# Another order of issue for a fused LSH-attention and token-mixing kernel, with a table of offsets

## The chip, the cores and the metric

The kernel runs on one core of a Trainium2 chip. The metric is device time in microseconds: 776.6 us before the change, the median of three runs (773.48, 776.6 and 777.08). The profile was taken from a further execution, which took 773.32 us.

The core has four engines that compute: TensorE (PE; PEld is its weight load), VectorE (DVE), ScalarE (ACT) and GpSimd (POOL). SyncE (SP) issues all transfers. Each engine runs its own queue in the order in which the program was written, and engines wait for each other by semaphores.

## The reference

Attention for 4 batches, 8 heads, 768 positions and width 64, in which a query sees only the keys whose six hash bits agree with its own; then, by batch, a token-mixing layer on the 512 joined channels.

```python
q_bucket = sum((q @ proj > 0) * powers);  k_bucket = sum((k @ proj > 0) * powers)
scores = where(q_bucket == k_bucket, q @ k.T / sqrt(64), -1e9)
x = softmax(scores) @ v                              # (4, 8, 768, 64) -> (4, 768, 512)
theta = x @ w_theta
y = w_tok_r @ (x * cos(theta)) + w_tok_i @ (x * sin(theta))     # over the 768 positions
u = x + y
out = u + relu(u @ w_ch)
```

## The kernel before

The work is cut into 96 attention steps, one for each batch, pair of heads and slice of 128 queries, and a mixing stage for each batch. Everything is first written down as some 3,300 small operations (`op(name, prio, ...)`, each with its engines, its rough length, what it depends on, and the buffers it holds). `issue_all` then plays a clock forward: whenever an engine is free in the model, it gives it the ready operation with the lowest `key`, and calls the function that writes the instructions. So the key, the model's lengths and the buffer counts decide the order in each engine's queue, and some operations (`qkl`, `p2`, `sign`, `zl` and others) go to whichever of two engines comes first.

One head of one attention step is this chain. TensorE makes the scores (`dst` for batch 0, one head at a time, from `nat`, `rows` and `kb`; `st` for the others, both heads, from `hl`). DVE takes the maximum (`vmax`, L800) and two small factors (L803, L806), ACT the exponential (`pf`, L810) and its 16-bit high half (`p1`, L816), POOL or DVE the low half (`p2`, L822). SP issues a transposing transfer (`turn`, L826, `pt<-pp`), and TensorE multiplies the result with the values (`pv`, 18 matmuls of 64 or 65 columns, `ps<-vv,pt`). The sums are divided into `x` (`norm`, L871).

Mixing for a batch transposes x (`xtr`, L921), projects it with `w_theta` (`proj`), turns the angles into sines on ACT (`trig`, L987 and L988), multiplies them with x on DVE (`zf`, tile `f`, L999), splits the products z into two halves (`zh`, `zl`, L1010), and runs the token mixing on TensorE (`y`, 36 matmuls for each of six output slices, `ps<-z,wtk`), which needs the z of all positions. Then come `u`, another projection with `w_ch`, and the store. The mixing of one batch runs among the attention steps of the next one; that of batch 0 thus starts after the 24 steps of batch 0.

The token weights (`raw`, then `wtk` at L520) and channel weights are loaded and split along the way. For batches 1 to 3 each pair of heads has its own preparation: q and k are split into two parts (`qkh`, and `qkl` at L631, tile `hl`), and their hash bits are made by TensorE, ACT and DVE, and turned into signs (`sign`, L707, tile `rows`) on DVE or POOL.

Where TensorE would have nothing to do in the model, and the model's clock is below `FILL`, the planner writes a filler, a 128x512 matmul of the constant tile `idle`, into the queue (`idle = e == "PE" and now < FILL ...`, L261, and `filler`, L354). Its result is not read. A filler in the queue runs whether the work behind it is ready or not.

Of the kernel before, what the change touches and what calls it, by code (L numbers as in the profile page):

```python
# [31 lines left out]
def lsh_attention_moe_kernel(ctx: ExitStack, tc: tile.TileContext, qk, wt, v, consts, w_theta, w_ch, out):  # L32
# [73 lines left out]
    WAKE = {"ACT": 45, "DVE": 37, "PE": 58, "POOL": 105, "SP": 40}  # L106
    AFTER = {"pv": 94, "vall": 70, "y": 17}
    WIDE = {"proj", "bits"}
    SHARED = {"qkl", "p1", "p2", "zf", "zh", "zl", "mag", "wlow", "whigh", "wmul", "wl", "vv2", "wtl"}

    class Slot:
        def __init__(self, pool):
# [26 lines left out]
    def issue_all():  # L139
# [1 line left out]
            return EXPORT(locals_())  # L141
        left = {}
        for i, o in enumerate(ops):
            o.key = (round(o.prio, 4), i)
            for sl in o.slots:
                left.setdefault(sl, []).append(o)

# [92 lines left out]
        while todo:  # L240
            progress = False
            for e in START:
# [165 lines left out]
    def widened(srcs, n, nm, tag, prio, stage="x", by=1.0):  # L408
        m = len(srcs)
        t = {}  # L410
        k_ = m * n / 512
        sx, sz = Slot(stage), Slot(tag)

        def load():
            t["w64"] = w64 = mp.tile([P, m, n, 2], U32, tag=sx.tag, name=f"w64_{nm}")
            for i, src in enumerate(srcs):
                dma(w64[:, i].rearrange("p n two -> p (n two)"), src)
            fs = mp.tile([P, 2, m, n], F32, tag=sz.tag, name=f"wf_{nm}")
            t["f"], t["sg"] = (fs[:, i].rearrange("p m n -> p (m n)") for i in range(2))
            t["w"] = fs[:, 0]  # L420
            w2 = w64.rearrange("p m n two -> p (m n) two")
            t["lo"], t["hi"] = w2[:, :, 0], w2[:, :, 1]

        def low():
            DVE.tensor_scalar(t["f"].bitcast(U32), t["lo"], 29, 0x40000000, ALU.logical_shift_right, ALU.bitwise_xor)

        def high():
            fu = t["f"].bitcast(U32)
            DVE.scalar_tensor_tensor(fu, t["hi"], 3, fu, ALU.logical_shift_left, ALU.bitwise_xor)

        a = op("wload", prio, on("SP", [(350, P * n * 8)] * m, load), slots=[sx, sz])
# [35 lines left out]
    def prep_wtok(to, prio):  # L467
# [4 lines left out]
        for r in range(2):  # L472
            def piece(r=r):
# [20 lines left out]
                a = op("wload", WL0 + WLS * (2 * to + r), on("SP", [(350, P * S * 8)], load), slots=[sw_])  # L494
# [40 lines left out]
    def prep_v(b, hp, prio):  # L535
# [42 lines left out]
        r = op("vload", prio + LV0, on("SP", [(410, 2 * S * D * 4)], load), slots=[svb])  # L578
# [16 lines left out]
    def prep_qk(b, hp, G, g):  # L595
# [10 lines left out]
                dma(t["nat"][:, i], qk[b, hp, :, i])  # L606

        if direct:
            hs.append(op("qkload", G + QKL, on("SP", [(330, 2 * S * D * 4)] * 2, whole), slots=[sh]))
        for i in range(0 if direct else 2):  # L610
            def half(i=i):
                sn = Slot("nat")
                u = {}

                def load():
                    u["nat"] = ap_.tile([P, S], F32, tag=sn.tag, bufs=1, name=f"nat{i}_{b}_{hp}")
                    dma(u["nat"], qk[b, hp, :, i])

                def high(e):
                    def go():  # L620
                        if "hl" not in t:
# [11 lines left out]
                ld = op("qkload", G + QKL + 0.02 * i, on("SP", [(330, 2 * S * D * 4)], load), slots=[sn])  # L633
# [102 lines left out]
    def step(g, b, hp, i, t, vt, po):  # L736
# [22 lines left out]
                        mm(st[j][:, k0:k1], l, r, n == 0, n == len(terms) - 1)  # L759

        if g < SH:
            a = [op("dst", g + DS * j, on("PE", 1750, lambda j=j: scores([j])), t["ready"], [ss[j]] + t["slots"]) for j in range(2)]
        else:
            a = [op("dst" if b == 0 else "st", g, on("PE", 1900 if b == 0 else 1600, lambda: scores([0, 1])), t["ready"], ss + t["slots"])] * 2

        def mcs():
            if "mc" not in mc:
                mc["mc"] = ap_.tile([P, 3, 2], F32, tag=smc.tag, bufs=1, name=f"mc_{nm}")
                order.extend((1, 0) if joint and ss[0].idx > ss[1].idx else (0, 1))
            return mc["mc"]  # L770

        order = []
# [1 line left out]
        def vmax2():  # L774
            a, c = sorted(x.idx for x in ss)
            DVE.tensor_reduce(mcs()[:, 0], psum[:, 2 * a * BANK : 2 * (2 * c - a) * BANK].rearrange("p (j n) -> p j n", j=2)[:, :, :S], AX.X, ALU.max, negate=True)

        def factor2():
# [5 lines left out]
        joint = g >= MG  # L784
        if joint:
            mj = op("vmax", g + VM, on("DVE", 1665, vmax2), [a[0], a[1]], ss + [smc])
            mj = op("factor", g + VM, on("DVE", 65, factor2), [mj], [smc])
            mj = op("shift", g + VM, on("DVE", 125, shift2), [mj], [smc])
        for j in range(2):
            def head(j=j):  # L790
# [55 lines left out]
                e = op("pf", gj + PF, on("ACT", 875, pf), [m], [ss[j], smc, spf], table="exp")  # L846
                k1 = op("p1", gj + KA, pick(g, P1, {"ACT": (733, p1("ACT")), "DVE": (470, p1("DVE"))}), [e], [spf, spp])
                k2 = op("p2", gj + KB, pick(g, P2, {"DVE": (870, p2(DVE)), "POOL": (1610, p2(POOL))}), [k1], [spf, spp])
                d = op("turn", gj + KT, on("SP", [(1475, 660000)], turn), [k2], [spp, spt])
                o_ = op("pv", gj + KV, on("PE", 560, pv), [d] + po["wait"] + po["all"][:1], [spt, po["slot"], vt["slot"], sx])  # L850
                po["all"].append(o_)

# [239 lines left out]
TAIL = ["m", "s"]  # L1092
WIN = {"x": 2, "hl": 2, "m": 3, "tmp": 3, "s": 3}
WRAW = ['wst', 'wst', 'z1', 'wst', 'wst', 'wst', 'wst', 'wst', 'wst', 'wst', 'wst']
WL0 = 44.531
WLS = 11.651
R0 = 1.082
SEP = 11.552
SH = 24
DS = 0.851  # L1100
MG = 999
ZH = 0
PF = -3.44
KA = 1.124
KB = -0.706
KT = 32.262
KV = 2.299
KN = 3.767
DJ = 0.156
VM = -5.147  # L1110
AB = -3.348
WTH = 15.173
WTS = -2.519
WC = 30.121
WCS = 3.108
# [5 lines left out]
TH0_3 = 0.273  # L1121
TH1_3 = 0.775
Y0_3 = 29.791
YS_3 = 3.092
Y1_3 = -0.034
PV0_0 = -0.991
QK0_0 = -0.742
QK1_0 = -66.594
HOLD = 0.361
FILL = 533350  # L1130
TH0_0 = 0.68
TH1_0 = -0.843
Y0_0 = 13.203
Y1_0 = 2.38
YS_0 = 8.904
PEN = 27.299
AHEAD = 1.701
H0 = -13.679
PST = 72.438
QKL = -17.525  # L1140
QK0 = 7.823
QK1 = -1.524
PV0 = -0.891
LV0 = 23.265
W0 = 6.042
WS = 5.025
TH0 = 0.752
TH1 = 0.891
Y0 = 10.192
YS = 6.684  # L1150
Y1 = 3.253
# [55 lines left out]
```

## Time and profile before

| | |
|---|---|
| median of three runs | 776.6 us (773.48 to 777.08) |
| the profiled execution's own time | 773.32 us |
| its span, first to last instruction | 771.5 us |
| mean granted TensorE clock | 0.974 |
| busy: PE, DVE, ACT, POOL | 745.0, 559.7, 526.2, 456.2 us |
| fillers | 163 |
| first token-mixing matmul at | 227.91 us |
| HBM read, written | 32.55 MB, 6.29 MB |

Busy time of PE holds the fillers too, and half-clock matmuls count with their longer time; it doesn't say how much of the span is useful work. The clock is 1 at 2.4 GHz and 0.5 at 1.2 GHz. A DMA share is that of the core's 16 DMA engines, and can come out a little over 1, as packets overlap.

### The profile page before, as it was taken

The page shows a single profiled execution, that of the slowest core. Times are in us where ns is not written, and L with a number is a line of the kernel's source. Part 1 is how long each engine was busy: PE and PEld are TensorE (multiplying, and loading weights), DVE is VectorE, ACT ScalarE, POOL GpSimd, SP SyncE. Part 2 cuts the span into 40 slices and gives each one's busy share as a digit, 9 for nine tenths or more (in the row PEclk, how much of TensorE's full clock was granted, in tenths as well). Part 3 has the DMA queues.
Part 4 walks back from the last instruction along what each step waited for, and adds up shares of the span by engine and source line. Part 5 has one row for each costly group of instructions (what it writes and reads, how often), then busy time and mean ns, then how long its engine had stood idle before and what let it go on. Part 6 is the DMA issues. An engine that isn't in the chain of part 4 may idle for free.

```text
span 771.5 us, 17408 instructions
## 1 busy us (share of the span) xinstructions
PE 745.0 (97%) x6819; PEld 498.4 (65%) x6819; DVE 559.7 (73%) x1170; ACT 526.2 (68%) x693; POOL 456.2 (59%) x320
## 2 busy tenths in 40 slices
PE   8998989999899999999999999999999999999997
PEld 3555555657656666787766666677756676775456
DVE  6796896959989878876998566578997555558023
ACT  3877597868987768667996666678995665567001
POOL 3755585674696577677777566567876655523000
PEclk9796999999989999999999999999999999999999
DMA  9599999997298799899566998798478698720002
GB/s 337 106 198 212 223 173 193 210 185 185 46 220 158 135 229 169 188 179 203 115 135 134 184 163 183 159 179 164 83 148 153 125 148 139 153 61 14 1 1 82
DMA packets 324570, 117.16 MB, mean 152 GB/s; under 512 B 309612, under 2 KB 313708, under 8 KB 324488
## 3 DMA queue, kind: packets, MB, share of 16 engines
q1 hardware_dynamic: 324488, 116.05, 74.4%
q8 instruction: 53, 0.87, 0.5%
q14 instruction: 29, 0.24, 0.1%
HBM read 32.55 MB, written 6.29 MB: 50 GB/s over the span
## 4 chain that ended last, share of the span: by engine, by line
PE 71%; DVE 9%; DMA 7%; ACT 7%; issue 3%; POOL 3%; SPq 1%; ACTq 0%; DVEq 0%; POOLq 0%
PE ps L96 68%; DMA pt<-pp 4%; DVE mc L800 3%; PE ps L921 2%; ACT pf L810 2%; ACT pp L816 2%; POOL pp L822 1%; DMA w_th<-in_moe_w_theta_dram 1%; POOL hl L631 1%; ACT L810 1%; DMA raw<-in_wt_dram 1%; DVE wtk L520 1%; DMA vrow<-vam 1%; DMA vamax<-vone 1%; DVE rows L707 1%
## 5 line engine op out<-in xcount | busy, mean ns | idle before, releaser
L822 POOL TENSOR_TENSOR pp<-pf,pp 128x768 f16<-128x768 f32 x189 | 324.6, 1734 | 169.0 <-ACT pp L816 146.7
L810 ACT ACTIVATE pf<-ps,mc 128x768 f32<-128x768 f32 x192 | 182.2, 988 | 122.8 <-DVE mc L806 98.5
L800 DVE TENSOR_REDUCE mc<-ps 128x1 f32<-128x768 f32 x192 | 176.7, 951 | 73.2 <-PE ps L96 71.3
L96 PE MATMUL ps<-z,wtk 128*128 128x512 f16 x864 | 203.5, 379 | 2.0 <-DVE x L1039 1.3
L816 ACT ACTIVATE pp<-pf 128x768 f16<-128x768 f32 x192 | 154.6, 840 | 11.2 <-DMA pt<-pp 11.0
L96 PEld LDWEIGHTS <-pt 128*128 128x128 f16 x3456 | 122.8, 99 | 41.0 <-issue 13.6
L96 PE MATMUL ps<-vv,pt 128*128 128x65 f16 (+1 forms) x3456 | 136.8, 195 | 6.3 <-DMA pt<-pp 6.3
L96 PEld LDWEIGHTS <-wtk 128*128 128x128 f16 x864 | 77.8, 98 | 85.4 <-issue 5.2
L96 PE MATMUL ps<-hl 64*128 64x512 f32 (+1 forms) x864 | 112.3, 354 | 4.1 <-ACT pf L810 4.1
L96 PE MATMUL ps<-kb,rows 64*128 64x256 f32 (+1 forms) x384 | 115.7, 425 | 0.0
L96 PEld LDWEIGHTS ps<-hl 64*128 64x128 f32 x864 | 75.7, 186 | 36.0 <-ACT pf L810 11.2
L96 PE MATMUL ps<-nat 64*128 64x512 f32 (+1 forms) x192 | 82.2, 563 | 2.6 <-ACT pf L810 2.5
L1010 POOL TENSOR_TENSOR z<-f,z 128x512 f16<-128x512 f32 x36 | 47.6, 1333 | 54.6 <-ACT z L1004 29.8
L96 PE MATMUL ps<-wch,h_u 128*128 128x512 f32 x192 | 63.3, 411 | 0.0
L96 PE MATMUL ps<-wth,h_x 128*128 128x512 f32 x192 | 62.7, 407 | 0.0
L96 PEld LDWEIGHTS ps<-kb,rows 64*128 64x128 f32 x384 | 50.3, 192 | 15.4 <-issue 10.6
L926 ACT ACTIVATE h_u<-ps 128x512 fp32r<-128x512 f32 x24 | 14.2, 597 | 59.2 <-PE ps L921 47.7
L999 DVE SCALAR_TENSOR_TENSOR f<-x,zsc,z 128x512 f32<-128x512 f32 x48 | 46.6, 995 | 5.6 <-ACT z L987 4.0
L96 PEld LDWEIGHTS ps<-nat 64*128 64x128 f32 x192 | 32.6, 205 | 26.0 <-issue 16.8
L96 PE MATMUL ps<-idle 128*128 128x512 f16 x163 | 45.9, 412 | 1.9 <-DVE ones L82 1.1
L96 PEld LDWEIGHTS ps<-wth,h_x 128*128 128x128 f32 x192 | 34.6, 189 | 8.4 <-issue 0.2
L96 PEld LDWEIGHTS ps<-wch,h_u 128*128 128x128 f32 x192 | 34.8, 189 | 8.0 <-DVE l_u L930 0.2
(112 smaller groups left out, 913.2 us busy)
## 6 DMA issues: line engine op xcount, KB each, us to landing
nat<-in_qk_dram SPq DMA_DIRECT2D x32, 384.0 KB
raw<-in_wt_dram SPq DMA_DIRECT2D x12, 768.0 KB
vb<-in_v_dram SPq DMA_DIRECT2D x16, 384.0 KB
out_dram<-x SPq DMA_DIRECT2D x24, 256.0 KB
pt<-pp SPq DMA_TRANSPOSE x192
w_th<-in_moe_w_theta_dram SPq DMA_DIRECT2D x4, 512.0 KB
w_ch<-in_moe_w_ch_dram SPq DMA_DIRECT2D x8, 256.0 KB
kb<-rows SPq DMA_DIRECT2D x30, 36.0 KB
```

The costliest lines, as they stand in the source:

```text
L96: PE.matmul(out_, l, r, start=start, stop=stop, skip_group_check=True)
L520: out_.append(op("wtl", prio, on("DVE", 930, lambda: DVE.scalar_tensor_tensor(lo16, t["f"], wsc[:, col], hi16, ALU.mult, ALU.subtract)), [ ...
L631: return lambda: eng.tensor_tensor(t["hl"][:, 1, i], u["nat"], t["hl"][:, 0, i].bitcast(F32), ALU.subtract)
L707: return lambda: eng.tensor_scalar(t["rows"][:56, lo : lo + n_], u["s"], affs[:56, 0:1], affs[:56, 1:2], ALU.is_ge, ALU.mult)
L800: DVE.tensor_reduce(col(0), st[j], AX.X, ALU.max, negate=True)
L810: ACT.activation(u["pf"], st[j], AF.Exp, bias=col(2), scale=col(1))
L816: ACT.activation(u["pp"][:, 0], u["pf"], AF.Copy)
L822: return lambda: eng.tensor_tensor(u["pp"][:, 1], u["pf"], u["pp"][:, 0], ALU.subtract)
L921: PE.transpose(u["pt"][:, c], src()[:, c * P : (c + 1) * P], ident)
L926: ACT.activation(u["hi"], u["pt"], AF.Copy)
L999: DVE.scalar_tensor_tensor(u["f"], tl[b][:, tt], zsc[:, b : b + 1], t["zw"][r][:, tt], ALU.mult, ALU.mult)
L1010: return lambda: eng.tensor_tensor(t["z"][r, 1][:, tt], u["f"], t["z"][r, 0][:, tt], ALU.subtract)
```

## The change

The lengths and sizes in the planner's model are set anew, its parameters (the priorities of kinds of operations) take other values, `FILL` is moved beyond the end of the model's clock, and the table `ADJ` gives 559 operations, named by their number, an offset to their priority. Every useful operation of before is still there, with the same instructions and the same buffers.

```diff
+    PAIR = {"dst": 860}
-    SHARED = {"qkl", "p1", "p2", "zf", "zh", "zl", "mag", "wlow", "whigh", "wmul", "wl", "vv2", "wtl"}
+    SHARED = {"qkl", "p1", "p2", "zf", "zh", "zl", "mag", "wlow", "whigh", "wmul", "wl", "vv2", "wtl", "sign", "scales"}
...
-            o.key = (round(o.prio, 4), i)
+            o.key = (round(o.prio + ADJ.get(i, 0), 4), i)
...
+                    if o.name == before and now - busy["PE"] < 60:
+                        dur -= PAIR.get(o.name, 0)
...
-                d = op("turn", gj + KT, on("SP", [(1475, 660000)], turn), [k2], [spp, spt])
+                d = op("turn", gj + KT, on("SP", [(1475, 720000)], turn), [k2], [spp, spt])
...
-WL0 = 44.531
+WL0 = 76.747
...
-KT = 32.262
+KT = 17.506
...
-FILL = 533350
+FILL = 917882
...
+ADJ = {
+    4: -7.6, 10: 1.23, 14: 2.16, 20: -1.9, 22: 0.08, 24: -1.11, 25: -0.02, 26: 0.13, 32: -0.76, 40: 5.35, 47: 1,
...
```

The model's sizes of the loads change in the same way (a load of q and k from 393,216 to 452,000, of a token weight from 786,432 to 904,000). A second form of `vmax` for both heads at once is added as well, but `MG`, `MG1` and `MGV` are all 999, above every step, so that it is not used.

Three places show what the order does. The first is TensorE around the first head's probabilities of step 5 (`pt0_0_0_5`; the last number counts tiles). Before, they stand right behind the scores:

```order
L96 MATMUL ps_72<-kb1_114,rows1_112 128x512
L96 MATMUL ps_72<-nat_0_1_125 128x256
L96 MATMUL ps_72<-kb1_114,rows1_112 128x256
L96 LDWEIGHTS pt0_0_0_5_637
L96 MATMUL ps_72<-vv_0_0_319,pt0_0_0_5_637 128x65
```

Now fillers stand between them, eleven pairs of the kind of the fourth and fifth row before the probabilities, and seven behind their 18 matmuls:

```order
L96 MATMUL ps_72<-kb1_114,rows1_112 128x512
L96 MATMUL ps_72<-nat_0_1_125 128x256
L96 MATMUL ps_72<-kb1_114,rows1_112 128x256
L96 LDWEIGHTS idle_84
L96 MATMUL ps_72<-idle_84 128x512
...
L96 LDWEIGHTS pt0_0_0_5_701
L96 MATMUL ps_72<-vv_0_0_321,pt0_0_0_5_701 128x65
```

In the whole program 269 fillers stand for 163, and ahead of the first token-mixing matmul 226 for 137.

The second place is DVE ahead of the last products of batch 0 (`f_0_0`, `f_0_1`, `f_1_0`; `rc` and `x` are the division of attention, `mc` the factors of a softmax). Before:

```order
L806 TENSOR_SCALAR mc_0_5_2659<-mc_0_5_2659 128x1 x2
L520 SCALAR_TENSOR_TENSOR wtk_97<-raw_1_2184,wsc,wtk_96 128x768
L704 TENSOR_TENSOR sum_1_2454<-ps,sum_1_2454 56x256
L555 TENSOR_REDUCE vone<-vrow 1x1
L707 TENSOR_SCALAR rows_112<-sum_1_2454,cst 56x256
L861 TENSOR_SCALAR rc_0_2_2739<-ps 128x6
L489 TENSOR_SCALAR raw_0_2657<-raw_0_2657 128x768
L864 RECIPROCAL rc_0_2_2739<-rc_0_2_2739 128x6
L999 SCALAR_TENSOR_TENSOR f_0_0_2773<-x_532,zsc,z_0_1791 128x512
```

And now, with line numbers that are 3 to 9 higher:

```order
L870 TENSOR_SCALAR rc_0_2_2791<-ps 128x6
L904 TENSOR_SCALAR swt<-winv,zinv 128x1
L873 RECIPROCAL rc_0_2_2791<-rc_0_2_2791 128x6
L880 SCALAR_TENSOR_TENSOR x_2798<-ps,vinv,rc_0_2_2791 128x3x128
L634 TENSOR_TENSOR hl_2_2683<-nat_1_2_2187,hl_2_2683 128x768
L407 TENSOR_SCALAR vinv<-vamax 128x1
L408 TENSOR_SCALAR vinv<-vinv 128x1
L409 TENSOR_SCALAR vsc<-vinv 128x1
L1008 SCALAR_TENSOR_TENSOR f_0_0_2844<-x_579,zsc,z_0_1384 128x512
```

The weight (`wtk<-raw`), the signs (`rows<-sum`) and the start of the next weight (`raw`, L489) are gone from here. The weight comes after the products, the signs have gone to POOL, and a split of `hl` and a division (`x_2798`) have come ahead of the products.

The third place is POOL at the same point of the program (`pp` are low halves of probabilities, `z0` and `z1` low halves of z). Before:

```order
L822 TENSOR_TENSOR pp0_1_0_4_2637<-pf0_1_0_4_2507,pp0_1_0_4_2637 128x768
L822 TENSOR_TENSOR pp1_1_0_4_2661<-pf1_1_0_4_2580,pp1_1_0_4_2661 128x768
L631 TENSOR_TENSOR hl_1_2_2670<-nat0_1_2_1997,hl_1_2_2670 128x768
L631 TENSOR_TENSOR hl_1_2_2670<-nat1_1_2_2020,hl_1_2_2670 128x768
L1010 TENSOR_TENSOR z0_0_1791<-f_0_0_0_2773,z0_0_1791 128x512
```

Now:

```order
L1019 TENSOR_TENSOR z1_0_1385<-f_0_3_1_2652,z1_0_1385 128x512
L710 TENSOR_SCALAR rows1_112<-sum_1_1_2533,cst_78 56x256
L831 TENSOR_TENSOR pp0_1_0_4_2730<-pf0_1_0_4_2543,pp0_1_0_4_2730 128x768
L831 TENSOR_TENSOR pp1_1_0_4_2754<-pf1_1_0_4_2586,pp1_1_0_4_2754 128x768
L634 TENSOR_TENSOR hl_1_2_2683<-nat1_1_2_2069,hl_1_2_2683 128x768
L1019 TENSOR_TENSOR z0_0_1384<-f_0_0_0_2844,z0_0_1384 128x512
```

One of the two splits of `hl` has left POOL for DVE, and the signs and two halves of z1 have come to it, ahead of the probabilities.

## Rows read from the trace of the kernel before

**Rows 1.** Page, parts 1 and 2: TensorE's busy time; granted clock in 40 slices.
```profile
PE 745.0 (97%) x6819; PEld 498.4 (65%) x6819; DVE 559.7 (73%) x1170; ACT 526.2 (68%) x693; POOL 456.2 (59%) x320
...
PEclk9796999999989999999999999999999999999999
```

**Rows 2.** Busy us (x instructions) by stretch, then granted clock, DMA share, GB/s.
```profile
0.00:40.00 40.00, 36.66 (x179) 19.82 (x180) 29.05 (x63) 23.09 (x31) 20.66 (x25) 0.87 0.73 227
40.00:80.00 40.00, 35.80 (x280) 22.43 (x279) 31.93 (x64) 27.77 (x36) 22.57 (x15) 0.79 0.99 203
80.00:160.00 80.00, 76.73 (x698) 46.91 (x697) 65.37 (x146) 62.87 (x81) 55.73 (x37) 0.98 1.02 194
160.00:228.00 68.00, 62.55 (x577) 44.23 (x576) 58.30 (x113) 59.62 (x80) 44.16 (x27) 0.95 0.72 152
228.00:320.00 92.00, 90.19 (x916) 56.98 (x915) 79.22 (x172) 66.79 (x100) 64.56 (x50) 1.00 0.92 183
320.00:668.00 348.00, 345.39 (x3618) 245.89 (x3615) 253.01 (x551) 252.72 (x322) 233.26 (x157) 1.00 0.80 153
668.00:772.00 104.00, 97.71 (x564) 62.11 (x562) 42.86 (x66) 33.37 (x50) 15.27 (x11) 0.99 0.16 39
```

**Rows 3.** The same view of the stretches at half clock, and their sum.
```profile
18.70:28.80 10.10, 10.10 (x25) 5.64 (x24) 6.85 (x16) 7.62 (x11) 7.71 (x5) 0.50 0.82 161
63.10:80.00 16.90, 15.40 (x111) 10.32 (x112) 11.02 (x26) 10.88 (x13) 7.56 (x4) 0.50 0.94 224
...
sum 36.80, PE 34.98 PEld 21.98 DVE 23.94 ACT 27.35 POOL 21.83; mean PE 8.74 PEld 5.49 DVE 5.99 ACT 6.84 POOL 5.46
```

**Rows 4.** The same view, instructions on the tile idle alone, up to 228 us.
```profile
0.00:228.00 228.00, 39.23 (x137) 12.50 (x137) 0.17 (x1) 0.92 0.87 189
```

**Rows 5.** TensorE in order of time: start, us, what; in brackets, the wait before.
```profile
17.15 1.12 PE L96 MATMUL ps<-nat 64*128 64x512 f32 x2 [2.02 <-ACT pf L810]
...
31.01 2.98 PE L96 MATMUL ps<-idle 128*128 128x512 f16 x13
33.92 1.12 PE L96 MATMUL ps<-nat 64*128 64x512 f32 x2
...
64.16 1.16 PE L96 MATMUL ps<-vv,pt 128*128 128x65 f16 x18 [2.04 <-DMA pt<-pp]
65.76 1.17 PE L96 MATMUL ps<-vv,pt 128*128 128x65 f16 x18 [0.44 <-DMA pt<-pp]
```

**Rows 6.** Chain that ended last, in order of time: start, us, what.
```profile
17.15 12.49 PE ps L96 x29
...
65.76 17.08 PE ps L96 x117
...
218.51 6.93 POOL hl L631 x2
...
303.19 5.82 DMA pt<-pp
```

**Rows 7.** All engines in order of time, before the first token-mixing matmul.
```profile
217.89 1.44 DVE L520 SCALAR_TENSOR_TENSOR wtk<-raw,wsc,wtk 128x768 f16<-128x768 f32 x1
...
218.47 6.96 POOL L631 TENSOR_TENSOR hl<-nat,hl 128x768 fp32r<-128x768 f32 x2
...
219.78 1.37 DVE L707 TENSOR_SCALAR rows<-sum,cst 56x256 fp32r<-56x256 f32 x1
220.75 1.04 ACT L988 ACTIVATE z<-z 128x1024 f32<-128x1024 f32 x1
...
225.49 0.45 PE L96 MATMUL ps<-hl,pst 128*64 128x512 f32 x1 [0.43 <-POOL hl L631]
...
227.91 2.32 PE L96 MATMUL ps<-z,wtk 128*128 128x512 f16 x10
```

**Rows 8.** Groups of instructions: the split of hl on DVE: busy us, mean ns.
```profile
L631 DVE TENSOR_TENSOR hl<-nat,hl 128x768 fp32r<-128x768 f32 x13 | 20.9, 1605 | 0.0
```

**Rows 9.** What SP's queue waited for: us in total, times, longest.
```profile
SPq L826 <- POOL pp L822: 152.1, 85, 6.5
```

More of the change, by code (lines that the diff above doesn't have):

```diff
@@ L429, in high @@
             DVE.scalar_tensor_tensor(fu, t["hi"], 3, fu, ALU.logical_shift_left, ALU.bitwise_xor)
-        a = op("wload", prio, on("SP", [(350, P * n * 8)] * m, load), slots=[sx, sz])
+        a = op("wload", prio, on("SP", [(350, 603000 * n // 512)] * m, load), slots=[sx, sz])
         b_ = op("wlow", prio, on("DVE", 80 + 270 * k_, low), [a], [sx, sz])
@@ L492, in high @@
                     DVE.scalar_tensor_tensor(t["lo"], t["hi"], 3, t["lo"], ALU.logical_shift_left, ALU.bitwise_xor)
-                a = op("wload", WL0 + WLS * (2 * to + r), on("SP", [(350, P * S * 8)], load), slots=[sw_])
+                a = op("wload", WL0 + WLS * (2 * to + r), on("SP", [(350, 904000)], load), slots=[sw_])
                 b_ = op("wlow", prio, on("DVE", 80 + 400, low), [a], [sw_])
@@ L576, in low @@
             DVE.scalar_tensor_tensor(t["vf"][:, :, W1 : W1 + D], src(), sc, t["vf"][:, :, :D], ALU.mult, ALU.subtract)
-        r = op("vload", prio + LV0, on("SP", [(410, 2 * S * D * 4)], load), slots=[svb])
+        r = op("vload", prio + LV0, on("SP", [(410, 452000)], load), slots=[svb])
         r = op("vamax", prio, on("DVE", 860, amax), [r], [svb])
@@ L608, in prep_qk @@
         if direct:
-            hs.append(op("qkload", G + QKL, on("SP", [(330, 2 * S * D * 4)] * 2, whole), slots=[sh]))
+            hs.append(op("qkload", G + QKL, on("SP", [(330, 452000)] * 2, whole), slots=[sh]))
         for i in range(0 if direct else 2):
@@ L631, in low @@
                     return lambda: eng.tensor_tensor(t["hl"][:, 1, i], u["nat"], t["hl"][:, 0, i].bitcast(F32), ALU.subtract)
[L633 removed]
+                ld = op("qkload", G + QKL + 0.02 * i, on("SP", [(330, 452000)], load), slots=[sn])
                 hs.append(op("qkh", pr, {"ACT": (735, high("ACT")), "DVE": (475, high("DVE"))} if g == 0 else on("ACT", 735, high("ACT")), [ld], [sn, sh]))
@@ L761, in step @@
         if g < SH:
-            a = [op("dst", g + DS * j, on("PE", 1750, lambda j=j: scores([j])), t["ready"], [ss[j]] + t["slots"]) for j in range(2)]
+            a = [op("dst", g + DS * j, on("PE", 1830, lambda j=j: scores([j])), t["ready"], [ss[j]] + t["slots"]) for j in range(2)]
         else:
-            a = [op("dst" if b == 0 else "st", g, on("PE", 1900 if b == 0 else 1600, lambda: scores([0, 1])), t["ready"], ss + t["slots"])] * 2
+            a = [op("dst" if b == 0 else "st", g, on("PE", 1750 if b == 0 else 1600, lambda: scores([0, 1])), t["ready"], ss + t["slots"])] * 2
         def mcs():
@@ L768, in mcs @@
                 mc["mc"] = ap_.tile([P, 3, 2], F32, tag=smc.tag, bufs=1, name=f"mc_{nm}")
-                order.extend((1, 0) if joint and ss[0].idx > ss[1].idx else (0, 1))
+                order.extend((1, 0) if joint and g >= MGV and ss[0].idx > ss[1].idx else (0, 1))
             return mc["mc"]
@@ L776, in vmax2, with vmax1 @@
             DVE.tensor_reduce(mcs()[:, 0], psum[:, 2 * a * BANK : 2 * (2 * c - a) * BANK].rearrange("p (j n) -> p j n", j=2)[:, :, :S], AX.X, ALU.max, negate=True)
+        def vmax1(j):
+            DVE.tensor_reduce(mcs()[:, 0, order[j] : order[j] + 1], st[j], AX.X, ALU.max, negate=True)
         def factor2():
@@ L782, in shift2 @@
             DVE.scalar_tensor_tensor(mcs()[:, 2], mcs()[:, 0], SHIFT, mcs()[:, 1], ALU.add, ALU.mult)
-        joint = g >= MG
+        joint = MG <= g < MG1
         if joint:
-            mj = op("vmax", g + VM, on("DVE", 1665, vmax2), [a[0], a[1]], ss + [smc])
-            mj = op("factor", g + VM, on("DVE", 65, factor2), [mj], [smc])
+            if g < MGV:
+                mj = [op("vmax", g + VM + DJ * j, on("DVE", 865, lambda j=j: vmax1(j)), [a[j]], [ss[j], smc]) for j in range(2)]
+            else:
+                mj = [op("vmax", g + VM, on("DVE", 1665, vmax2), [a[0], a[1]], ss + [smc])]
+            mj = op("factor", g + VM, on("DVE", 65, factor2), mj, [smc])
             mj = op("shift", g + VM, on("DVE", 125, shift2), [mj], [smc])
@@ L1094 @@
 WRAW = ['wst', 'wst', 'z1', 'wst', 'wst', 'wst', 'wst', 'wst', 'wst', 'wst', 'wst']
-WL0 = 44.531
-WLS = 11.651
-R0 = 1.082
-SEP = 11.552
+WL0 = 76.747
+WLS = 8.786
+R0 = 2.044
+SEP = 11.659
 SH = 24
-DS = 0.851
+DS = 0.77
 MG = 999
+MG1 = 999
+MGV = 999
 ZH = 0
-PF = -3.44
-KA = 1.124
-KB = -0.706
-KT = 32.262
[L1107 to L1115, printed above, removed]
+PF = -3.964
+KA = 1.188
+KB = -0.51
+KT = 17.506
+KV = 1.816
+KN = 7.125
+DJ = 0.654
+VM = -4.923
+AB = 9.988
+WTH = 15.563
+WTS = -2.423
+WC = 32.082
+WCS = 2.729
 P1 = [[0, 999, ['ACT']]]
@@ L1120 @@
 GROUPS = [[(0, 3), (3, 6)], [(0, 4), (4, 6)], [(0, 2), (2, 4), (4, 6)]]
[L1121 to L1126, printed above, removed]
-QK0_0 = -0.742
-QK1_0 = -66.594
-HOLD = 0.361
-FILL = 533350
[L1131 to L1151, printed above, removed]
+TH0_3 = -0.456
+TH1_3 = 0.993
+Y0_3 = 34.663
+YS_3 = 15.788
+Y1_3 = -0.048
+PV0_0 = -2.078
+QK0_0 = -0.742
+QK1_0 = -69.744
+HOLD = 0.364
+FILL = 917882
+TH0_0 = 0.472
+TH1_0 = -0.067
+Y0_0 = 13.072
+Y1_0 = 2.222
+YS_0 = 9.945
+PEN = 26.308
+AHEAD = 1.919
+H0 = -29.844
+PST = 95.879
+QKL = -14.167
+QK0 = 90.846
+QK1 = 0.073
+PV0 = 2.139
+LV0 = 3.454
+W0 = 5.686
+WS = 5.469
+TH0 = 0.987
+TH1 = 0.788
+Y0 = 9.406
+YS = 6.017
+Y1 = 3.384
+ADJ = {
[63 rows of a table added]
+}
 EXTRA_INT = {"SEP": [0, 12, 20, 24, 30], "WRAW": [["wst"] * 12, ["z1"] + ["wst"] * 10, ["wst", "wst", "z1"] + ["wst"] * 8], "MG": [999], "ZH": [0, 1], "BUFS": [dict(hl=2, rows=2, sum=1, mc=3, pf=a, pp=b_, pt=c, vb=1, tmp=3) for a, b_, c in ((2, 3, 3), (3, 4, 4), (2, 4, 5), (3, 5, 3), (3, 3, 5), (2, 5, 4))]}
```

62 rows, old and new, of the table ADJ are left out of this document.

## Prediction

> **What bounds the kernel now.** I read the page first, then the busy time by stretch, the chain that ended last, and the instructions just ahead of the first token-mixing matmul. The page [rows 1] shows TensorE busy for 97% of the span. That is not 97% useful work: 163 matmuls on the tile `idle` (fillers, whose result nobody reads) count as busy. The stretches [rows 2] show two kernels in one. From 228 us on, TensorE waits 1.8 us up to 320, 2.6 up to 668 and 6.3 in the tail, all at full clock. Before 228 us, while attention of batch 0 runs and the angles of its mixing follow, it waits 16.3 us (the sum of what the first four rows leave), and four stretches run at half clock, 1.2 for 2.4 GHz [rows 3]: 36.8 us, in which it is busy 35.0, so that up to 17.5 us are lost. No other engine is full there (DVE 73 to 86%), and the DMA share is about 1 from 40 to 160 us.
>
> So the change must pay in the first 228 us or nowhere: behind them TensorE has few holes to fill, and the useful matmuls are the same.
>
> **The change part by part.** No useful instruction is added or removed; the order, the engine of a few (where the planner may choose) and the number of fillers change. In the new order 269 fillers stand for 163. Ahead of the first token-mixing matmul there are 226 for 137 [rows 4]. Eleven more stand behind it, nine of them where the chain is at about 310 us. Six come after the last useful matmul and cost nothing, since only additions and stores are left, which don't wait for TensorE.
>
> *Price of a filler.* Thirteen in a row begin at 31.01 us and the next matmul at 33.92 [rows 5]: 0.22 us each at full clock. The 89 early ones cost 19.6 us of TensorE. If every wait and all half clock of the first part went, the first token-mixing matmul, now at 227.9 us [rows 7], could come 16.3 + 17.5 - 19.6 = 14.2 us earlier. If no wait went, and all 89 stood in front of ready work, it would come 19.6 us later. These are the ends; the value between depends on where the fillers stand.
>
> *The clock.* Two of the half-clock stretches lie under pieces of the chain that are TensorE itself [rows 6]: 12.49 us from 17.15, of which 18.7 to 28.8 ran at half clock (10.1 us), and 17.08 us from 65.76, of which all up to 80.0 did (14.2 us). At full clock they would shrink by half, 5.1 + 7.1 = 12.2 us. A wait stands at the head of both: 2.02 us before 17.15, and 2.04 and 0.44 before the probabilities' matmuls at 64.16 and 65.76 [rows 5]. The new order puts 11 fillers directly before and 7 directly behind the first of these two, about 4 us, and 13, 12 and 11 between score operations at the other place, so I expect full clock through both pieces. But what follows each is a softmax and a transpose, and with a DMA share near 1 matmuls that are done earlier will partly wait for transposes that are not. I take 5 of the 12.2 us; the ends are 0 and 12.2.
>
> The Trainium skill, "TensorE: Matmul & The Clock Gate" (Terms, and Part 1), prices the throttle at its time multiplied by one minus the clock's share, and in another place puts the ramp under 1% of a typical span and advises against modelling it. By the first, 18.4 us would come back instead of my 5, and the sum below would read 753; by the second the fillers would buy next to nothing. The trace agrees with neither as it stands: 17.5 us are 2.3% of the span, but only 12.2 of them lie on the chain.
>
> *The last stretch before token mixing.* The first of these matmuls needs z of its rows: sines on ACT, products on DVE, their halves on DVE and POOL. In the trace [rows 7] DVE spends 1.44 us on a weight (`wtk`) and 1.37 on signs (`rows`) just ahead of the last products, and POOL runs two `hl` splits, 6.96 us, from 218.47; the matmul at 225.49 waited for the second, and POOL's own z halves are queued behind it. In the new order the weight stands behind the products, the signs have gone to POOL (earlier), and one `hl` split has gone to DVE. So DVE has 2.8 us less and 1.6 more [rows 8]; POOL has half of 6.96, 3.5 us, less at the critical place, against the signs and two z halves that it takes up earlier. The chain goes through POOL here [rows 6], so I take 3 us. The ends are 0 (the sines run to 221.8 on ACT [rows 7] and may be late next) and 3.5.
>
> *Fillers that are too many.* The 36 between the first score operations cost 7.9 us, against 2.0 us of waiting and 5.1 us of half clock that they replace; that leaves 0.8 us, and I put 1 us on the loss side for all runs. The ends are 0 and the 9.8 of the last rival below.
>
> *After 228 us.* The nine fillers at about 310 us cost up to 2.0 us; the chain has a transpose there, 5.82 us from 303.19 [rows 6], and TensorE waits in that stretch anyway. Whatever else is rearranged moves under a TensorE that is busy without a break; if that cover had a hole, it would show as a wait of the kind that now adds up to 4.4 us between 228 and 668 [rows 2]. I take 0, with ends at -3 and +2.
>
> **Sum.** -5 - 3 + 1 + 0 = -7 us. The profiled execution took 773.3 us (span 771.5, and 1.8 around it), so 766.3. The median of the three runs shown is 776.6, 3.3 above the profiled one; I keep that offset and forecast 769.6, rounded to 769.5 us.
>
> **Rivals.**
> *All waits filled.* Every filler takes the place of a wait. Then 14.2 us come off the first part and 1 later: 758.1, with the offset 761.4. For it: before 228 us TensorE loses 33.8 us to waits and clock, more than the 19.6 that the new fillers cost. Against it: the DMA share of 1.
>
> *The transposes bind.* The work up to some 160 us is timed by the transposes that SP issues. Their order is almost the same in both (loads move by a few transposes at most), so fillers just replace waiting, and only the last stretch pays: -3 + 1, 771.3, with the offset 774.6, which can't be told from no change. For it: shares of 0.99 and 1.02 [rows 2]. Against it: SP stood for 152.1 us in all, 85 times, because POOL's second halves were not there yet [rows 9], so the queue was often empty. The Trainium skill, "Perfetto Trace Analysis" (What "DMA-bound" means), names a solid issuing track as one sign of a bound by DMA; by SP's row that sign is missing, which takes a little from this rival.
>
> *Fillers in front of ready work* (the slower side). TensorE runs its queue in order, and a run of 10 to 17 fillers takes 2 to 4 us even where the scores behind it are ready. Later scores make a later softmax and a later transpose, so the waits move and do not shrink. If half of the 89 stand so, they add 9.8 us; with the last stretch's 3 off, 780.1, with the offset 783.4. It decides from about 8 us of such fillers on, when they eat the 5 and the 3. For it: 100 fillers more are the one thing that is certain to take TensorE's time. Against it: the runs whose place I looked up stand where the trace has waits.
>
> **How the numbers follow.** Forecast 0.48 (its own range 764 to 775), all waits filled 0.17, transposes bind 0.20, fillers in the way 0.15. A difference under about 0.5%, 3.9 us, can't be told from none: 772.7 to 780.5. Faster are four fifths of the forecast, all of the second and a fifth of the third: 0.38 + 0.17 + 0.04, rounded 0.6. Slower is the last, 0.15. The rest, 0.25, is no change. The range from 758 to 783 leaves out about one in ten at each end.
>
> **What would show it.** Right: the clock row is full from 20 us on but for one short stretch at most; TensorE's waits before the first token-mixing matmul fall from 16.3 to under 8 us; that matmul begins at 219 to 224 us; and from it to the end of the span it takes within 2 us of today's 771.5 - 227.9 = 543.6. Wrong: the first token-mixing matmul at 228 us or later, where waits of 0.4 to 2 us still before the probabilities' matmuls speak for the transposes, and none there for fillers in the way. Also wrong: a time from there to the end that differs by more than 3 us, since the gain or loss would then be in the part that I take as saturated.

## The result and the profile after

The changed kernel takes 768.57 us (median of five runs, 767.95 to 770.46) where the kernel before took 776.6 in five runs beside it (773.48 to 777.11). The ratio is 0.9898, with an interval of 0.9864 to 0.9932: 8 us or 1% faster. The forecast was 769.5. But the two profiled executions, 769.92 and 773.32 us, are only 3.4 us apart. The profile of before is one of its shorter executions, and what the other 4.6 us are made of has to come from more profiles than these two. In all ratios, executions that lie more than 1.5% above the fastest one of the same kernel are left out.

The page answers to [rows 1]. TensorE is busier by 9.8 us, and the clock row has one 8 left:

```profile
PE 754.8 (98%) x6925; PEld 501.8 (65%) x6925; DVE 560.7 (73%) x1173; ACT 525.0 (68%) x690; POOL 452.1 (59%) x320
...
PEclk9999899999999999999999999999999999999999
```

By stretch (columns as in [rows 2]), TensorE now waits 8.8 us before 228 us, for 16.3:

```profile
0.00:40.00 40.00, 38.56 (x210) 20.37 (x211) 31.37 (x63) 24.00 (x32) 20.52 (x25) 1.00 0.82 245
40.00:80.00 40.00, 36.63 (x304) 22.16 (x302) 34.39 (x76) 28.79 (x40) 24.30 (x17) 0.92 0.96 197
80.00:160.00 80.00, 79.98 (x731) 49.98 (x730) 59.15 (x140) 61.50 (x78) 54.42 (x37) 0.98 0.97 192
160.00:228.00 68.00, 64.03 (x581) 44.36 (x580) 52.50 (x103) 58.30 (x76) 42.70 (x30) 0.97 0.70 140
228.00:320.00 92.00, 91.49 (x919) 56.92 (x918) 79.37 (x169) 67.35 (x100) 67.84 (x50) 1.00 0.91 183
320.00:668.00 348.00, 347.03 (x3655) 247.43 (x3652) 259.76 (x560) 254.44 (x324) 229.76 (x156) 1.00 0.84 156
668.00:768.00 100.00, 97.11 (x544) 60.57 (x540) 44.20 (x68) 30.66 (x45) 12.61 (x9) 1.00 0.16 35
```

Two stretches at half clock are left of four, 13.2 us for 36.8 [rows 3]; the same view:

```profile
73.60:83.60 10.00, 8.17 (x49) 5.08 (x48) 6.12 (x16) 7.19 (x10) 5.45 (x6) 0.50 1.04 201
203.30:206.50 3.20, 3.20 (x9) 2.36 (x8) 2.38 (x7) 3.17 (x4) 0.17 (x1) 0.50 0.04 0
```

The fillers before 228 us, which answer to [rows 4], hold TensorE for 56.79 us, 17.6 more:

```profile
0.00:228.00 228.00, 56.79 (x226) 20.65 (x226) 0.17 (x1) 0.97 0.86 187
```

TensorE in order of time at the second place of [rows 5]. The fillers stand where the waits of 2 us were. Waits of 0.59 and 0.95 us stand a little later, ahead of the fall of the clock at about 73.5, and one of 1.83 behind it:

```profile
59.28 2.55 PE L96 MATMUL ps<-idle 128*128 128x512 f16 x11
61.66 0.71 PE L96 MATMUL ps<-vv,pt 128*128 128x65 f16 x18
62.21 1.67 PE L96 MATMUL ps<-idle 128*128 128x512 f16 x7
...
67.52 0.73 PE L96 MATMUL ps<-vv,pt 128*128 128x65 f16 x18 [0.59 <-DMA pt<-pp]
...
71.03 1.12 PE L96 MATMUL ps<-nat 64*128 64x512 f32 x2 [0.95 <-ACT pf L819]
...
77.21 1.16 PE L96 MATMUL ps<-vv,pt 128*128 128x65 f16 x18 [1.83 <-DMA pt<-pp]
78.30 2.07 PE L96 MATMUL ps<-nat 64*128 64x512 f32 x2
```

The chain up to the first token-mixing matmul answers to [rows 6]. It is TensorE in longer pieces, with transposes in between; POOL's `hl` is gone from it, and a small broadcast (`vamax`, the scale of a batch's values) has come to its end:

```profile
8.66 36.61 PE ps L96 x239
...
68.11 9.05 DMA pt<-pp
...
77.21 57.53 PE ps L96 x511
...
207.57 5.42 DMA pt<-pp
...
218.28 3.98 DMA vamax<-vone
```

All engines ahead of that matmul, as in [rows 7]:

```profile
217.10 1.94 DVE L634 TENSOR_TENSOR hl<-nat,hl 128x768 fp32r<-128x768 f32 x1
...
218.18 2.54 POOL L634 TENSOR_TENSOR hl<-nat,hl 128x768 fp32r<-128x768 f32 x1
...
219.34 1.04 ACT L997 ACTIVATE z<-z 128x1024 f32<-128x1024 f32 x1
...
222.28 0.15 DVE L407 TENSOR_SCALAR vinv<-vamax 128x1 f32<-128x1 f32 x1 [3.25 <-DMA vamax<-vone]
...
223.64 0.72 PE L96 MATMUL ps<-vv,pt 128*128 128x65 f16 x18 [0.46 <-DMA pt<-pp]
...
226.55 2.81 PE L96 MATMUL ps<-z,wtk 128*128 128x512 f16 x12
```

The sines end at 220.4 us instead of 221.8, but DVE stands 3.25 us for the broadcast before it starts the last products. The split of `hl` on DVE takes 1.94 us here ([rows 8] had a mean of 1.6), and SP still waits 147.5 us for POOL's halves (152.1 in [rows 9]).

A mark inside the first part will be needed below: the last pair of `h_x` matmuls of the projection with `w_theta`. It starts at 203.79 us before,

```profile
203.79 0.62 PE L96 MATMUL ps<-wth,h_x 128*128 128x512 f32 x2
```

and at 205.58 after:

```profile
205.58 1.05 PE L96 MATMUL ps<-wth,h_x 128*128 128x512 f32 x2
```

So the 3.4 us of the two profiles are +1.8 up to that mark, -3.1 from there to the first token-mixing matmul (24.1 to 21.0), and -2.0 behind it (543.6 to 541.5).

### The profile page after: what moved, and what is told of

Read it like the earlier page. It is cut to its first block, busy times and chain, and to the rows that moved or that the text cites. A ratio compares the mean times of both kernels' runs of the same rounds, so it can differ in the third digit from the quotient of the medians.

```text
span 768.1 us, 17610 instructions
## 1 busy us (share of the span) xinstructions
PE 754.8 (98%) x6925; PEld 501.8 (65%) x6925; DVE 560.7 (73%) x1173; ACT 525.0 (68%) x690; POOL 452.1 (59%) x320
## 4 chain that ended last, share of the span: by engine, by line
PE 83%; DVE 5%; DMA 5%; ACT 3%; issue 2%; POOL 1%; SPq 1%; ACTq 0%; DVEq 0%; POOLq 0%
PE ps L96 81%; DMA pt<-pp 4%; PE ps L930 3%; DVE mc L809 2%; ACT pf L819 1%; DVE f L1008 1%; ACT pp L825 1%; DMA vamax<-vone 1%; POOL pp L831 0%; DVE wf_ch L441 0%; POOL z L1019 0%; ACT L819 0%; DMA vrow<-wmx 0%; DVE mc L815 0%; DVE mc L812 0%
## 5 line engine op out<-in xcount | busy, mean ns | idle before, releaser
L831 POOL TENSOR_TENSOR pp<-pf,pp 128x768 f16<-128x768 f32 x187 | 320.4, 1731 | 168.7 <-ACT pp L825 151.4
L96 PE MATMUL ps<-z,wtk 128*128 128x512 f16 x864 | 205.8, 379 | 0.1
L96 PEld LDWEIGHTS <-pt 128*128 128x128 f16 x3456 | 121.6, 98 | 42.4 <-issue 13.4
L96 PE MATMUL ps<-hl 64*128 64x512 f32 (+1 forms) x864 | 109.0, 351 | 0.6 <-ACT pf L819 0.6
L96 PE MATMUL ps<-kb,rows 64*128 64x256 f32 (+1 forms) x384 | 109.3, 411 | 0.0
L96 PEld LDWEIGHTS ps<-hl 64*128 64x128 f32 x864 | 72.9, 184 | 30.8 <-issue 8.1
L1019 POOL TENSOR_TENSOR z<-f,z 128x512 f16<-128x512 f32 x38 | 50.9, 1350 | 57.1 <-DVE z L1015 28.7
L96 PE MATMUL ps<-nat 64*128 64x512 f32 (+1 forms) x192 | 76.4, 517 | 1.0 <-ACT pf L819 1.0
L96 PE MATMUL ps<-idle 128*128 128x512 f16 x269 | 67.6, 391 | 1.1 <-DVE ones L82 1.1
L96 PEld LDWEIGHTS ps<-kb,rows 64*128 64x128 f32 x384 | 46.7, 186 | 14.3 <-issue 9.7
L96 PEld LDWEIGHTS ps<-nat 64*128 64x128 f32 x192 | 30.6, 190 | 20.2 <-issue 13.2
L96 PEld LDWEIGHTS <-idle 128*128 128x128 f16 x269 | 24.3, 100 | 28.9 <-issue 5.9
```

Source lines behind the costliest of these rows:

```text
L96: PE.matmul(out_, l, r, start=start, stop=stop, skip_group_check=True)
L831: return lambda: eng.tensor_tensor(u["pp"][:, 1], u["pf"], u["pp"][:, 0], ALU.subtract)
L1019: return lambda: eng.tensor_tensor(t["z"][r, 1][:, tt], u["f"], t["z"][r, 0][:, tt], ALU.subtract)
```

## The experiments

In every experiment the planner is replaced by a list, each operation with its engine and its buffers, in the order in which one of the two planners had issued them; a filler is an entry of that list. So order and fillers can be set apart. The short diffs show entries of TensorE around the place of the prediction (`pv 348` is the probabilities' matmuls of step 5; the numbers count operations), as a count where entries repeat. Line numbers differ from those above: L97 is the matmul helper and L729 the transposition of x.

**The old order with the new fillers**, put ahead of the same operations as in the new kernel:

```diff
 dst 432
+filler x11
 pv 348
 pv 356
 dst 433
+filler x7
 pv 384
```

> The order of before, word for word, with the fillers of the new order, each run of them ahead of the same operation (269 fillers). Theory 'order': the first part is timed by chains outside TensorE, the fillers only fill its waits, and what the change gains comes from the order of the later part; then 773 to 778 us, first token-mixing matmul at 226 to 230 us. Rival 'clock': the fillers are the gain, since they hold the full clock; then 767 to 771 us, and first token mixing at 220 to 224. Rival 'in the way': 784 us or more, with first token mixing past 235.

It took 785.25 us, 1.0129 of before (1.0098 to 1.0159); first token-mixing matmul at 236.9 us, as the rival 'in the way' had it. **The new order with the old fillers**, the other way round:

```diff
 dst 412
-filler x11
 pv 348
-filler x7
 pv 384
```

> The new order, with the 163 fillers of before, each run ahead of the same operation as there. 'Order': 767 to 771 us, as with all fillers, though half clock comes back in the first 228 us. 'Clock': 774 to 778 us. 'In the way': 758 to 764 us, as some of the 100 fillers' 22 us come back.

798.57 us, 1.0303 (1.0262 to 1.0343); that matmul at 254.9, and 64.9 us at half clock. None of the three expectations holds. Neither part alone brings the gain, but both kernels carry a flaw: the eleven (here ten) fillers of the start slid behind the first hash bits, and the start is 3 to 5 us late. So they were made anew, a filler now standing ahead of the operation with the same number in TensorE's row. **Old order, new fillers by place:**

```diff
 dst 432
+filler x11
 pv 348
+filler x7
 pv 356
```

> The order of before with the new order's fillers, now by place: a run that stands ahead of TensorE's n-th operation there stands ahead of the n-th here (in e1 some slid behind the first hash bits, which were then 4 us late). 'Fillers and order belong together' (a run pays only in front of the wait it was planned for): 778 to 783 us, first token mixing at 230 to 234. 'Clock' (fillers pay wherever they fall, as long as they keep the clock): 767 to 772. 'Fillers are free in the first part': 774 to 777.

779.2 us, 1.0019 (0.9989 to 1.0049). The clock was up but for 6.8 us (mean 0.996), and TensorE's waits before the token mixing fell to 13.4 us, yet that matmul came at 234.0, 6 us later than in the profile of before (the medians are 2.6 apart). In this order the clock that returns does not pay for the fillers that bring it, as 'belong together' had it. **New order, old fillers by place** (of the eleven and the seven none, as above):

> The new order with the 163 fillers of before, by place. 'Fillers and order belong together': 780 to 792 us, with 40 us and more of half clock before the first token mixing. 'Clock' says the same here, 780 or more. 'Order': 766 to 771, since the waits of the first part take the fillers' place.

793.94 us, 1.0202 (1.0154 to 1.025), that matmul at 249.3, 61.4 us at half clock in three stretches. With the old fillers for its own the new order loses 25 us against the new kernel.

**No fillers at all**, in the new order:

```diff
 dst 412
-filler x11
 pv 348
-filler x7
 pv 384
```

> The new order without one of its 269 fillers. Theory (order and fillers were found together, and this order needs its fillers for the clock): TensorE runs at half clock in the first part for 40 to 80 us as in the run with the old fillers (54 to 65 us there), the first token-mixing matmul comes at 240 to 260 us, and the time is 785 to 800 us. Rival (only misplaced fillers hurt, none would do as well): the first token-mixing matmul within 3 us of 226 and the time 766 to 772 us.

and in the old one (the five fillers ahead of `dbits 490` are the last before that place):

```diff
-filler x5
 dbits 490
 dbits 492
 dst 393
```

> The order of before without its 163 fillers. Theory (the old order leans on its fillers too, but on fewer): more half clock than the 36.8 us of before, first token-mixing matmul at 232 to 245 us, time 780 to 790 us, so less of a loss than the new order without its own. Rival (the first part is timed by transposes, TensorE waits at either clock): within 3 us of before, 773 to 779 us.

1.0358 of before (1.0257 to 1.0459) and 1.0121 (1.0009 to 1.0233). Each ratio rests on two executions, and the spread is wide: the new order took 798.4 and 808.0 us (and 811.2 and 811.4), the old one 779.2 and 790.5 (and 801.7 and 801.8). The lower the mean clock, the longer most of them are: 0.918 at 798.4, 0.907 at 808.0, 0.952 at 779.2, 0.909 at 801.7. The profile of the new order (808.0 us) has its first token-mixing matmul at 263.7, and its clock of 0.907 means some 150 us at half clock, for the 40 to 80 that were expected. Its clock row:

```profile
PEclk9586775565897999999999999999999999999999
```

The profile of the old order (801.7 us, one of those left out) has that matmul at 255.2, later than the 232 to 245 expected. By these few executions the old order loses some 8 us or more without its 163 fillers, the new one 35 or more without its 269, and by itself the new order is the worse of the two.

Order and fillers side by side, in us (medians; without fillers the mean of the two executions that count):

| | no fillers | the old fillers | the new fillers |
|---|---|---|---|
| old order | 784.8 | 776.6 | 779.2 |
| new order | 803.2 | 793.9 | 768.6 |

The new order beats the old one with its own fillers only, and the old order gains nothing from the new fillers. They have to be judged as a pair.

**The first part of one kernel with the rest of the other**, cut ahead of the first token-mixing matmul (`y 2437`); all issued before it follows the one list, the remainder the order of the other:

```diff
-list of before
+list of before up to y 2437, then the list of the new kernel
```

> Before's order and fillers up to the first token-mixing matmul, the new ones for all that is left then. 'Order of the later part is the gain': 769 to 773 us, with 538 to 541 us from the first token-mixing matmul to the end of the span. 'The first part is the gain' (the prediction): 774 to 777 us, and 543 to 545 us for the rest.

774.18 us, 0.999 (0.9959 to 1.0022), which fits the prediction's reading. The first part of before, but for two fillers at its end, took 230.5 us this time, against 227.9 in before's profile, so it varies by some 2.6 us by itself. The rest took 542.4, which lies between the two readings. The other cut:

```diff
-list of the new kernel
+list of the new kernel up to y 2437, then the list of before
```

> The new order and fillers up to the first token-mixing matmul, before's for all that is left then. 'Order of the later part is the gain': 773 to 776 us, first token mixing at 226 to 228. 'The first part is the gain': 769 to 771 us, as in the timed runs the first part of before may take longer than in its profiled one.

777.62 us, 1.0025 (1.0003 to 1.0047), which fits neither reading: the first part was short (225.5), but 7 us were lost right behind the cut, where TensorE waits 4.3 us for DVE at 233.45. That the work which the new first part had put off falls on the old rest there is an inference. The hybrids also give buffers out anew, which nothing here controls for. By time, then, neither half alone brings a gain that stands clear of the noise; the shares below come from profiles.

**The value scale later**, to take away DVE's wait of 3.25 us; the scale goes behind the last products on DVE, and the broadcast behind two transposes on SP:

```diff
-DVE vscale 899
 DVE zf 2399
 ...
 DVE zf 2408
+DVE vscale 899
...
-SP vbc 898
 SP turn 849
 SP turn 857
+SP vbc 898
```

> The new order and fillers, but the value scale (vinv and vsc on DVE) stands behind the last four products of batch 0, and its broadcast on SP behind the two transposes of that step. In the new kernel DVE waits 3.25 us there for the broadcast, ahead of the products. If that wait is what ate the prediction's 3 us of the last stretch: first token mixing 1 to 3 us earlier, 766 to 768 us. If TensorE's own queue (transposes, scores) sets that point: within 0.5 us of the new kernel, 768 to 769.

768.94 us (768.65 to 770.15), 0.9891 (0.9852 to 0.9931), first token-mixing matmul at 225.5. The wait ended the chain, but the time is the same without it, and from the mark to the first token-mixing matmul it takes 20.8 us for 21.0. **Half of the fillers of the middle**, from step 9 to the transposition of x (43 fewer):

```diff
 dst 670
-filler x6
 filler x7
 dst 690
```

> The new order, with every second filler left out from the first probabilities of step 9 to the first angle projection (85 become 42; TensorE waits 0.02 us in all from 80 to 160 us there). 'In the way': up to 9 us come off, 760 to 765. 'Fillers only fill waits, and hold the clock': waits take their place, 767 to 772, and more if half clock returns (over 772).

769.59 us (768.01 to 774.01), 0.9904 (0.9865 to 0.9943), that matmul at 224.7: TensorE's waits before it go from 8.8 to 15.8 us, so waits come where fillers stood, and the time is the same. **Both together:**

> The new kernel with both earlier edits: the value scale and its broadcast behind the last products, and every second filler of the middle of the first part left out (226 to 269 fillers, 43 fewer). Theory (each wait that goes leaves another one that ends as late): 767 to 770 us, the same as the new kernel. Rival (DVE's wait and the fillers covered for each other): first token-mixing matmul at 221 to 223 us and 763 to 766 us.

772.22 us (767.73 to 777.97), 0.9947 (0.9908 to 0.9986), that matmul at 227.2. That is above both ranges. In its profile a wait of 1.87 us for an exponential at 130.56, behind a halved run of fillers, goes with 10.2 us of half clock from 130.9 on, where the new kernel has full clock, so fillers can also be too few. No version beats the new kernel.

**More transfers** in the new kernel:

```diff
 dma(w, wt[2 * to + r].bitcast(U32))
+NLOAD.append(1)
+n = len(NLOAD) - 5
+if 0 <= n <= 3:
+    dma(out[3 - n // 2].rearrange("(p t) d -> p (t d)", t=T)[:, n % 2 * 2 * S : (n % 2 + 1) * 2 * S].bitcast(U32), wt[2 * to + r].bitcast(U32))
```

> The new kernel with four more transfers of 786 KB each, right behind four of its token weight loads between 66 and 135 us, from the weights to a part of the output that is written over at the end, so that nothing waits for them: 3.1 MB read and 3.1 MB written, at the 200 GB/s of this stretch 15 us of the transfer engines for the read alone. Theory (the transposes set the pace of the first part, with a DMA share near 1): the first token-mixing matmul goes from 226 to 236 to 256 us, TensorE's waits for pt grow by 10 to 25 us, the time is 779 to 798 us. Rival (TensorE with its fillers sets the pace, and the DMA share of 0.97 is not full): the first token-mixing matmul within 3 us of 226 and the time 767 to 773 us.

778.22 us (776.2 to 782.99), 1.0009 of before (0.9969 to 1.005), so some 9 us slower than the new kernel and just under the theory's 779. In its profile (782.7 us, a long one) the first token-mixing matmul starts at 239.6, 13 us later. TensorE's waits for transposes grow only from 4.3 to 9.3 us,

```profile
PE ps L97 <- DMA pt<-pp: 9.3, 5, 4.2
```

but behind a wait of 1.68 us that ends at 154.0 the clock falls, and stays down with TensorE busy throughout. Of the 13 us, TensorE's waits of all kinds make 6 (14.8 for 8.8) and its longer busy time 7:

```profile
154.60:175.00 20.40, 20.40 (x106) 12.06 (x103) 6.64 (x20) 9.61 (x12) 9.22 (x7) 0.50 0.70 124
```

So late transposes do delay this first part, which speaks for the theory, though their waits stay under the 10 to 25 us that it asked for.

## Why the prediction came out right, and where it was not

*The sum is right, its terms are not.* It put -5 for the clock, +1 for fillers that are too many, -3 for the last stretch and 0 behind 228 us. That the time came out as forecast is in good part luck: the clock with its fillers gave about 1 us of 4, and 3 us came from where the prediction had put nothing.

*The clock (-5, with +1 for fillers): mis-sized.* The clock came back as forecast, to within 13.2 us at half clock. What became of it shows in TensorE's busy time up to the first token-mixing matmul, before:

```profile
0.00:227.91 227.91, 211.65 (x1729) 133.31 (x1730) 184.56 (x382) 173.27 (x225) 143.03 (x103) 0.92 0.87 189
```

and after:

```profile
0.00:226.55 226.55, 217.75 (x1814) 136.19 (x1815) 176.22 (x378) 171.14 (x221) 140.57 (x105) 0.97 0.86 186
```

Fillers are 39.1 us of the first and 56.8 of the second. So the waits fall by 7.5 us and the useful matmuls take 11.6 less (172.5 and 161.0; 1.3 of it is work put off, see below), but the fillers take 17.7 more, and 1.4 us are left. The term that failed is the +1: fillers cost ten us more than the waits whose place they took, and that is most of what the clock gave back. Up to the last projection the profiled pair gained nothing (+1.8). Over the profiles in which each order has its own fillers (the new one's whole or halved), the mark lies at 203.8 and 206.8 us (old first part), and at 201.9 to 206.3 (new first part, five profiles, mean 204.4): -1 us, for the -4 of the two terms, and less than either group spreads. The prediction's reason for taking only 5 of 12.2, that matmuls done earlier wait for transposes that are not, fits this, though of the 8.8 us of waits that are left only 4.3 are for transposes. In the old order the whole return of the clock buys nothing: the new fillers take 18.8 us more there, the waits fall by 2.8, and the first token mixing comes 6 us later.

*The last stretch (-3): the size right, the reason not.* From the mark to the first token-mixing matmul it takes 23.7 to 25.8 us in the four profiles with the old first part and fillers in it, and 20.5 to 22.8 in the nine with the new one, whatever fillers stand there (none to 44). The prediction took the 3 us from weights and signs on DVE and from POOL's `hl`. But TensorE waited for `hl` only 0.43 us [rows 7]. What it lost in this stretch, before:

```profile
208.76 0.49 PE L96 MATMUL ps<-hl 64*128 64x512 f32 x1 [1.88 <-ACT pf L810]
210.22 1.65 PE L96 MATMUL ps<-hl 64*128 64x512 f32 x5 [0.97 <-ACT pf L810]
...
224.12 0.94 PE L96 MATMUL ps<-hl,pst 128*128 128x512 f32 x3
```

and after:

```profile
213.03 0.72 PE L96 MATMUL ps<-vv,pt 128*128 128x65 f16 x18 [0.88 <-DMA pt<-pp]
...
229.01 1.28 PE L96 MATMUL ps<-hl,pst 128*128 128x512 f32 x4
```

Two waits for exponentials, 2.9 us, are gone, for two of 0.9 and 0.5 us for transposes; and four matmuls of hash bits, 1.3 us, which stood ahead of the first token mixing, now stand behind it, so that this part of the 3 us is only put off. The waits for exponentials (1.7 to 1.9 and 0.9 to 1.0 us) and the early hash bits stand in all five profiles with the old first part, the waits in none with the new one; the hybrid that has the early bits without the waits takes 22.0 us. The old order with the new fillers has as many fillers here as the new kernel (42, 9.9 us) and full clock, and still takes 23.7 us. So it is the order; which of its moves does it was not tried. The new wait of DVE, which the chain shows and the prediction did not foresee, takes little of it, as the run with the later scale shows.

*Behind the first token-mixing matmul (0, ends -3 and +2): mis-sized.* The rest takes 543.6 to 546.1 us in the three profiles with the old order throughout and fillers, and 540.5 to 542.8 in the nine that end with the new one: -3 us. The cover had holes after all. They lie in one place. The token mixing of the second and third batch begins at the same time in both profiles of the pair (380.0 and 380.3, 544.5 and 544.4 us): the 1.4 us by which the first came earlier are gone by then, with the put-off hash bits and the additional fillers in between. That of the last batch begins at 695.88 before and at 692.03 after. TensorE between the third and the last, before and after, with as many matmuls and no filler:

```profile
544.54:695.88 151.34, 147.87 (x1511) 103.96 (x1511) 100.94 (x215) 102.71 (x132) 87.25 (x58) 1.00 0.71 129
544.39:692.03 147.64, 147.32 (x1511) 103.40 (x1511) 103.29 (x217) 101.96 (x132) 85.41 (x57) 1.00 0.75 132
```

This stretch takes 150.1 to 151.8 us in the five profiles that end with the old order and 147.5 to 147.8 in the nine that end with the new one, whatever stood ahead. What TensorE waited for there (us in total, times, longest), before:

```profile
PE ps L921 <- DVE l_x L930: 1.9, 1, 1.9
PE ps L96 <- ACT pf L810: 1.0, 3, 0.4
PE ps L96 <- DVE x L1039: 0.6, 1, 0.6
```

and after:

```profile
PE ps L96 <- ACT pf L819: 0.3, 1, 0.3
```

3.5 us of waits fall to 0.3. The largest single one, the transposition of x of the last batch at 677.87 us, which waits for DVE, stands in every profile that ends with the old order. In the one with the new fillers by place:

```profile
PE ps L729 <- DVE l_x L738: 1.9, 1, 1.9
```

and in none that ends with the new order. So it goes with the order, not with the fillers; no run moves this one operation alone. The prediction had read the 6.3 us of waiting in the tail [rows 2] and not asked what they were.

*The sum by runs.* -1, -3 and -3 make -7, for 8 between the medians, but the first is less than its spread, and the profiles of before differ by 2.6 us in the first part alone. Of the 8 us only the 2 to 4 between the third and the last token mixing stand clear in every profile; how much the first part adds stays open. The offset of 3.3 us that was added to the profiled time did not carry over: the new kernel's profile lies 1.4 above its median. The forecast of the median was near because the profile of before was a short one and its gain of 3.4 us a small one.

*The rivals.* All waits filled: fell, since 8.8 us of waits are left and the half of the fillers that was taken out in the middle only turned into waiting. Fillers in front of ready work: fell for the new order (43 fewer fillers gain nothing), but it describes the new fillers in the old order, where they make it no faster at full clock. The transposes bind: close for the time up to the last projection, where neither the clock nor fewer fillers moved the end and the run with more transfers did, though half of its delay was the clock. It had nothing for the rest.

*What was to show it.* Half clock was to be one short stretch and is two; waits under 8 us are 8.8; the first token-mixing matmul at 219 to 224 came at 226.55; the rest, within 2 us of 543.6, is 2.0 lower, just at its bound. The first three miss narrowly and in one direction: the first part gained less than forecast.

## What to carry to other kernels

Ask of a filler whether it stands in front of the wait that it was planned for: the new fillers in place of the old ones are worth 25 us in the order that they were made with and nothing in the other, so an order and its fillers are compared as a pair only. A clock that returns is not yet time saved: here most of it went to the fillers that brought it. Look past the first matmul of a stage as well, since a gain up to there can be work put off. And where an engine is busy for 97% and more, list the waits that are left one by one: here five of 0.3 to 1.9 us in the last batch are the part of the gain that every profile shows.

## What the runs showed of the hardware

Half clock outlasts the wait before it. In the new order without fillers TensorE waited 1.69 us for a transpose up to 112.5 us, fell to 1.2 GHz, and stayed there for 51 us in which it was busy but for 0.5, with scores of 64 rows and the probabilities' 64 or 65 columns:

```profile
112.90:164.00 51.10, 50.65 (x313) 33.21 (x311) 21.41 (x59) 26.18 (x32) 24.07 (x17) 0.50 0.74 164
```

It rose at 164.0, behind eight matmuls of 128 rows and 512 columns (hash bits) and 18 of the probabilities, without any filler. In the run with more transfers it stayed down for 20.4 us, with TensorE busy for all of them, and rose at 175.1, behind four fillers and at the start of seven more. In both stretches TensorE hardly waits, so the view of waits does not show the loss.

Half clock does not double every matmul's time. Two score matmuls go from 1.12 to 2.07 us, but the 18 of the probabilities only from 0.71 to 1.16 (the rows at 61.66, 71.03, 77.21 and 78.30 above). So taking half of the time at half clock as lost, as the prediction did, is a bound from above.

The same DMA share stands for different rates. Two slices of 2.5 us, in the run with more transfers and in the new kernel, with the whole of 60 to 160 us of each (the last two numbers are the share and GB/s):

```profile
60.00:160.00 100.00, 90.55 (x784) 56.18 (x783) 72.62 (x164) 69.90 (x91) 60.53 (x40) 0.92 1.02 218
70.00:72.50 2.50, 1.99 (x8) 1.12 (x7) 2.43 (x7) 2.37 (x3) 0.52 (x1) 1.00 1.02 398
60.00:160.00 100.00, 96.61 (x862) 60.11 (x861) 77.14 (x181) 75.44 (x97) 64.88 (x43) 0.95 0.99 196
135.00:137.50 2.50, 2.50 (x44) 2.06 (x39) 2.50 (x6) 1.26 (x2) 1.71 (x2) 1.00 1.09 390
```

At a share of about 1 the slices reach 398 and 390 GB/s, about twice the mean of the 100 us around them, so a share of 1 is not a full rate in bytes. With 3.1 MB more to copy, the mean rose only from 196 to 218 GB/s. Which kinds of transfers make the difference, no run here separates.
